# Softcapped attention and a gated MLP in one kernel: score tiles of 64 keys of two head pairs, 64x64 products, another order of steps

## The chip, the cores and the metric

The kernel runs on one core of a Trainium2 chip. The metric is device time in microseconds (us) of one execution. PE is TensorE, ACT is ScalarE, DVE is VectorE, POOL is GpSimd; SP issues transfers. L315 and the like are line numbers of the kernel before.

## The reference

```
q, k, v: (4, 12, 448, 64) float32; cap = 30; w_in (768, 2048), w_out (2048, 768)
scores = q @ k.T / sqrt(64)
scores = cap * tanh(scores / cap)
attn = exp(scores - max(scores))
attn = attn / (sum(attn) + 1e-9)
x = (attn @ v), heads side by side: (1792, 768)
h = x @ w_in
out = (h * sigmoid(h)) @ w_out
```

## The kernel before

The kernel has two parts: attention, then the MLP (called MoE in the code). Weights arrive as 64-bit floats and are turned into 32-bit ones by steps on DVE ("decode", lines L167 to L180).

**Attention.** Batch and heads make 24 head pairs; a *slot* s treats two pairs, t = 0 and 1, which is four heads, and there are 12 slots. A pair has its queries and keys, transposed, in one tile QK (128 partitions: head e of the pair on partitions 64e to 64e+63; three buffers), and its values in VT. The 448 keys of a head are cut into three chunks of 128 and a rest of 64.

- `qk(i, j)` (L315): the scores of pair i and key chunk j. Four products of 64x64 weights with 448 columns fill one score tile: partitions are the chunk's 128 keys, the two halves are the heads. `qk_rem(s)` (L327) does the last 64 keys of both pairs of the slot in one tile. Score tiles have three buffers of two PSUM banks each, and the tile of the sums takes one of them in turn.
- `tanh` (L337, L341) reads a score tile out of PSUM and writes the weights P; `exp` (L345) works in place: chunks 0 and 1 of a pair together (1792 elements a partition), chunk 2 (896), and the rest of both pairs (896).
- `pv(i, j)` (L378): values of a chunk, two products of 128x64 into the value tile O, one PSUM tile of two banks with a single buffer. `pv_rem` (L386): the rest, four products of 64x64.
- `sums` (L355, L360) adds the weights of the chunks on DVE into T, one tile a pair; `fold` (L390) adds the rest by two accumulating transfers on POOL's queue; `pv_sum` (L400) sums over the keys by products with a tile of ones, 128x32 each, into 448 columns of a score tile, two slots late.
- `u_vals` (L407) copies O out of PSUM, which frees it. `u_sums` (L415 to L429) turns the sums by a transpose on DVE, takes the reciprocal, turns them back, and sends them to the partitions of both halves by eight transfers. `norm` (L440 to L444) multiplies and writes the result as a high and a low part, XH and XL.

The order of attention is written out by hand. `SLOT` is a list of such steps, run for each slot; `-1` or `+1` behind a name is the slot before or the next one. Each engine has its own queue and takes its instructions in this order; what is late holds up what stands behind it on its engine. `ENDS` are lists for the last slots, into which six pieces of the MLP's first unit (H0 to H5) are put. `FIRST` says which slot does which decode step.

**MLP.** w_in is applied by a Strassen-like scheme (`chain`, L745), w_out by `o_unit` (L855). Each product is done as three, of high and low parts. PE's order here is a fixed line; `plan` orders the work of the other engines by costs and due times, from assumed times at which they come free. The result is added up in DRAM by accumulating transfers (L897).

Loads of QK, VT and the rest values VB are issued on POOL's queue (L299, L302, L306), those of the first slot on SP's.

Of the kernel before, what the change touches and what calls it, by code (L numbers as in the profile page):

```python
# [185 lines left out]
def tile_softcap_attention_swish_moe(  # L186
# [40 lines left out]
    W02 = [const.tile([128, 2 * DM], F32R, name=f"w{r}") for r in range(3)]  # L227
# [16 lines left out]
    QK = [a1.tile([128, S + KW], F32, name=f"QK{r}") for r in range(3)]  # L244
# [35 lines left out]
    O = {}  # L280
    U = {}
# [13 lines left out]
    def load_rem(b, eng=nc.gpsimd):  # L295
# [5 lines left out]
    def load_qk(i, eng=nc.gpsimd, c0=0, c1=S + KW):  # L301
        eng.dma_start(out=QK[i % 3][:, c0:c1], in_=qkv[i, :, c0:c1])  # L302

    def load_v(s, eng=nc.gpsimd):
        for t in range(2):
            eng.dma_start(out=VT[s % 2][:, t], in_=qkv[2 * s + t, :, S + KW:])  # L306

    def qk(i, j):

        q = QK[i % 3]  # L310
        ps = scores_tile()
        for c in range(2):
            for e in range(2):
                k0 = S + 128 * CHUNK[j] + 64 * c
                nc.tensor.matmul(  # L315
                    ps[half(c), e, 0:S], q[half(e), k0:k0 + 64], q[half(e), 0:S], start=True, stop=True
                )
        SP[i, j] = ps

    def qk_rem(s):  # L320

        ps = scores_tile()
        for t in range(2):
            q = QK[(2 * s + t) % 3]
            for e in range(2):
                k0 = S + KF + 64 * e
# [3 lines left out]
        SP[s, "r"] = ps  # L330

    def tanh(i, j):
        t = i % 2
        if (i, j // 2) not in P:
            P[i, j // 2] = a1.tile([128, 4 - j, S], F32, tag=f"P{t}{j // 2}", name="P")
        p = P[i, j // 2][:, 2 * (j % 2):2 * (j % 2) + 2]
        nc.scalar.activation(out=p, in_=SP.pop((i, j))[:, :, 0:S], func=AF.Tanh, scale=REG["sct"])  # L337

    def tanh_rem(s):
        P[s, "r"] = a1.tile([128, 2, S], F32, tag="PR", name="P", bufs=2)  # L340
        nc.scalar.activation(out=P[s, "r"], in_=SP.pop((s, "r"))[:, :, 0:S], func=AF.Tanh, scale=REG["sct"])  # L341

    def exp(i, h):
        p = P[i, h]
# [5 lines left out]
    def sums(i, n):  # L350

        p = P[i, n]
        if n == 0:
            T[i] = a1.tile([128, 2, S], F32, tag=f"T{i % 2}", name="T", bufs=2)
            nc.vector.scalar_tensor_tensor(  # L355
                out=flat(T[i]), in0=flat(p[:, 0:2]), scalar=epst[:, 0:1], in1=flat(p[:, 2:4]),
                op0=ALU.add, op1=ALU.add,
            )
        else:
            nc.vector.tensor_tensor(flat(T[i]), flat(T[i]), flat(p), ALU.add)  # L360

    CHUNK = (1, 2, 0)
    DONE = {}

    def summed(i):
        if i // 2 not in O:
            O[i // 2] = ps_o.tile([128, 2, 512], F32, tag="o", name="o")
        n = DONE[i] = DONE.get(i, 0) + 1
        return n == 1, n == KC + 1

    def pv(i, j):

        s, t = divmod(i, 2)
        start, stop = summed(i)
        for e in range(2):
            v = VT[s % 2][:, t, D * (e * KC + CHUNK[j]):D * (e * KC + CHUNK[j]) + D]
            p = P[i, j // 2][:, 2 * (j % 2) + e]
            nc.tensor.matmul(O[s][half(e), t, 0:S], v, p, start=start, stop=stop)  # L378

    def pv_rem(s):  # L380
        for t in range(2):
            start, stop = summed(2 * s + t)
            for e in range(2):
                v = VB[(s // NU) % 2][half(t), s % NU, e]
                p = P[s, "r"][half(t), e]
                nc.tensor.matmul(O[s][half(e), t, 0:S], v, p, start=start, stop=stop)  # L386

    def fold(s):
        for t in range(2):
            nc.gpsimd.dma_start(out=T[2 * s + t][half(t)], in_=P[s, "r"][half(t)], accum_op=ALU.add)  # L390

    def pv_sum(s, folded=True):

        ps = scores_tile()
        for z in (1,) if folded else (0, 1):
# [16 lines left out]
    def u_sums(s, parts=(0, 1, 2)):  # L412
        if 0 in parts:
            UW[s] = au.tile([128, S // 32, 32], F32, tag="US", name="US", bufs=2)
            nc.vector.transpose(flat(UW[s]), US.pop(s)[:, 0, 0:S])  # L415
        if 1 in parts:
            CW[s] = au.tile([128, S // 32], F32, tag="CS", name="CS", bufs=1)
            nc.vector.reciprocal(out=CW[s], in_=UW[s][:, :, 0])
        if 2 not in parts:
            return  # L420
        u = UW.pop(s)
        nc.vector.transpose(u, CW.pop(s).unsqueeze(2).to_broadcast([128, S // 32, 32]))
        rt = flat(u)

        r = au.tile([128, 2, S], F32, tag="R", name="R", bufs=2)
        for e in range(2):
            for h in range(2):
                for c in range(2):
                    nc.sync.dma_start(  # L429
                        out=r[64 * e + 32 * h:64 * e + 32 * h + 32, c], in_=rt[64 * e + 32 * c:64 * e + 32 * c + 32]  # L430
                    )
        RB[s] = r

    def norm(s, parts=(0, 1, 2)):
        b, u = s // NU, s % NU
        cs = slice(b * S, (b + 1) * S)
        x = U[s]
# [43 lines left out]

    def step(op, sh, slot):
        s = slot + sh
        if not 0 <= s < NS:
            return
        i = 2 * s + (1 if op[1:2] == "k" else 0)
        j = int(op[2]) if op[2:3].isdigit() else None
        if op == "SUM":
            pv_sum(s, s + 1 < NS)
        elif op == "UC":  # L490
            u_vals(s)
        elif op[:2] == "UT":
            u_sums(s, (j,))
        elif op[0] == "N":
            norm(s, (int(op[1]),))
        elif op[0] == "D":
            if (slot, op) in FIRST:
                decode(*FIRST[slot, op])
        elif op == "A":
            if s + 1 < NS:  # L500
                fold(s)
        elif op == "L1":
            if s + 1 < NS:
                load_qk(2 * s + 3)
# [824 lines left out]
```

## Time and profile before

| | |
|---|---|
| median of 3 runs | 606.33 us (605.38 to 607.08) |
| profiled execution | 605.26 us, span 603.4 us |
| granted clock of PE over the span | 0.999 |
| PE busy | 594.9 us (99%), 3578 products |
| DVE busy | 425.8 us (71%) |
| ACT busy | 370.0 us (61%) |
| POOL busy | 225.5 us (37%) |
| PE's first score product | 4.16 us |
| PE's first MLP product behind attention | 153.62 us |

Busy shares are means over both parts. In the page's slices ACT is at 9 tenths or more in nearly all of attention and at about 5 in the MLP, so attention has to be read by itself. A product of 32-bit numbers shows as two records on PE, one for each pass.

### The profile page before, as it was taken

The numbers are of one execution on the slowest core, as the hardware profiler recorded it, in microseconds if no ns is written. First come the engines' busy times: TensorE is split into PE (matmuls) and PEld (weight loads), VectorE is DVE, ScalarE is ACT, GpSimd is POOL, SyncE is SP. The second block draws the span as 40 slices with busy tenths as digits, with TensorE's granted clock in tenths as the row PEclk, the third lists the DMA queues.
The fourth block names the chain that finished last, engine by engine and source line by source line (L and its number), as shares of the span: only waits on it lengthen the run. The fifth ranks groups of instructions, "written<-read, shape, count | busy, mean of one in ns | idle before, by whom it ended". The sixth has DMA issues, their size and how long they took to land.

```text
span 603.4 us, 9839 instructions
## 1 busy us (share of the span) xinstructions
PE 594.9 (99%) x3578; PEld 477.8 (79%) x3578; DVE 425.8 (71%) x703; ACT 370.0 (61%) x602; POOL 225.5 (37%) x300
## 2 busy tenths in 40 slices
PE   7999999999999999999999999999999999999996
PEld 3333333334899999999999999999999999999996
DVE  2779888789888898766756585766676575747653
ACT  7999999997356565655655554645556555545120
POOL 2354433420043214433643463444335434635210
PEclk9999999999999999999999999999999999999999
DMA  7799999974394627988897899789898978998875
GB/s 249 209 221 215 256 209 183 239 161 66 67 309 122 209 100 140 141 172 184 120 202 97 181 138 201 101 192 147 158 175 127 200 103 178 134 198 138 287 244 199
DMA packets 46698, 105.13 MB, mean 174 GB/s; under 512 B 8018, under 2 KB 33746, under 8 KB 46642
## 3 DMA queue, kind: packets, MB, share of 16 engines
q0 software_dynamic: 33312, 67.62, 63.1%
q1 hardware_dynamic: 13330, 36.81, 18.1%
q8 instruction: 30, 0.49, 0.4%
q14 instruction: 26, 0.21, 0.1%
HBM read 47.97 MB, written 44.04 MB: 152 GB/s over the span
## 4 chain that ended last, share of the span: by engine, by line
PE 96%; ACT 2%; DVE 1%; issue 0%; ACTq 0%; DVEq 0%
PE q L855 38%; PE A L745 15%; PE C L745 10%; PE o L378 8%; PE s L315 8%; PE B L745 6%; PE D L745 4%; PE s L400 2%; PE o L386 1%; PE s L327 1%; ACT P L345 1%; ACT P L337 1%; PE s L745 1%; PE o L262 0%; DVE T L355 0%
## 5 line engine op out<-in xcount | busy, mean ns | idle before, releaser
L897 POOL DMA_DIRECT2D out_dram<-st x196 | 163.2, 964 | 252.4 <-ACT st L599 231.7
L855 PE MATMUL q<-w,gh 128*128 128x376 f32 (+1 forms) x876 | 187.6, 335 | 0.0
L855 PEld LDWEIGHTS q<-w,gh 128*128 128x128 f32 x876 | 156.4, 188 | 2.8
L599 ACT ACTIVATE st<-q 128x376 f32<-128x376 f32 (+1 forms) x184 | 82.6, 489 | 66.6 <-PE q L855 54.3
L855 PE MATMUL q<-w,gl 128*128 128x376 f32 (+2 forms) x438 | 111.3, 335 | 0.0
L855 PEld LDWEIGHTS q<-w,gl 128*128 128x128 f32 x438 | 80.2, 188 | 0.0
L345 ACT ACTIVATE P<-P 128x896 f32<-128x896 f32 (+1 forms) x60 | 71.2, 1259 | 0.0
L337 ACT ACTIVATE P<-s 128x896 f32<-128x896 f32 x72 | 62.4, 925 | 5.8 <-PE s L315 5.7
L315 PE MATMUL s<-QK 64*64 64x448 f32 x576 | 60.3, 545 | 2.1 <-ACT P L337 1.1
L745 PE MATMUL A<-XH,w 128*128 128x384 f32 (+1 forms) x192 | 60.5, 359 | 0.0
L378 PE MATMUL o<-P,VT 128*64 128x448 f32 x288 | 56.8, 543 | 0.0
L315 PEld LDWEIGHTS s<-QK 64*64 64x64 f32 x576 | 20.1, 133 | 39.5 <-issue 13.3
L599 ACT ACTIVATE gh<-gf 128x512 fp32r<-128x512 f32 (+1 forms) x63 | 36.3, 578 | 21.5 <-DVE gf L809 21.5
L815 DVE TENSOR_TENSOR gl<-gf,gh 128x512 fp32r<-128x512 f32 (+1 forms) x63 | 39.1, 622 | 13.3 <-ACT gh L599 13.2
L378 PEld LDWEIGHTS o<-P,VT 128*64 128x64 f32 x288 | 19.6, 137 | 36.0 <-issue 30.7
L599 ACT ACTIVATE gf<-A 128x512 f32<-128x512 f32 (+1 forms) x34 | 18.7, 549 | 42.6 <-PE A L745 39.6
L745 PE MATMUL C<-XH,w 128*128 128x384 f32 (+1 forms) x136 | 41.0, 363 | 0.0
L355 DVE SCALAR_TENSOR_TENSOR T<-P,epst 128x896 f32<-128x896 f32 x24 | 26.9, 1123 | 17.9 <-ACT P L345 17.9
L390 POOL DMA_DIRECT2D T<-P x22 | 18.6, 845 | 54.1 <-ACT P L345 34.8
L169 ACT ACTIVATE gf<-RAW 128x384 f32<-128x384 f32 x56 | 30.6, 548 | 13.1 <-DVE C L827 4.9
L745 PE MATMUL A<-xt,w 128*128 128x512 f32 (+1 forms) x168 | 38.3, 363 | 0.0
L745 PEld LDWEIGHTS A<-XH,w 128*128 128x128 f32 x192 | 35.6, 188 | 3.3
(136 smaller groups left out, 933.3 us busy)
## 6 DMA issues: line engine op xcount, KB each, us to landing
out_dram<-st POOLq DMA_DIRECT2D x98, 196.0 KB, 4.9
out_dram<-st POOLq DMA_DIRECT2D x98, 188.0 KB, 4.0
RAW<-in_moe_w_in_dram SPq DMA_DIRECT2D x15, 768.0 KB, 6.2
RAW<-in_moe_w_out_dram SPq DMA_DIRECT2D x14, 768.0 KB, 7.3
QK<-in_qkv_dram POOLq DMA_DIRECT2D x21, 480.0 KB, 5.2
R<-US SPq DMA_DIRECT2D x96, 56.0 KB, 4.1
T<-P POOLq DMA_DIRECT2D x22, 224.0 KB, 4.5
VT<-in_qkv_dram POOLq DMA_DIRECT2D x22, 192.0 KB, 4.6
```

Of the source, the lines that this page charges most:

```text
L169: nc.scalar.activation(out=tmp, in_=high.bitcast(F32), func=AF.Abs)
L315: nc.tensor.matmul(ps[half(c), e, 0:S], q[half(e), k0:k0 + 64], q[half(e), 0:S], start=True, stop=True)
L337: nc.scalar.activation(out=p, in_=SP.pop((i, j))[:, :, 0:S], func=AF.Tanh, scale=REG["sct"])
L345: nc.scalar.activation(out=p, in_=p, func=AF.Exp, scale=REG["cap"])
L355: nc.vector.scalar_tensor_tensor(out=flat(T[i]), in0=flat(p[:, 0:2]), scalar=epst[:, 0:1], in1=flat(p[:, 2:4]), op0=ALU.add, op1=ALU.add,)
L378: nc.tensor.matmul(O[s][half(e), t, 0:S], v, p, start=start, stop=stop)
L390: nc.gpsimd.dma_start(out=T[2 * s + t][half(t)], in_=P[s, "r"][half(t)], accum_op=ALU.add)
L599: nc.scalar.activation(out=out, in_=in_, func=AF.Copy)
L745: nc.tensor.matmul(ps, w(a), x(b), start=(first and z == 0), stop=(last and z == 2), skip_group_check=more)
L815: nc.vector.tensor_tensor(gl, gf, gh.bitcast(F32), ALU.subtract)
L855: nc.tensor.matmul(pe(e), g[a][:, ts], w[:, b, cols[e]], start=(z == 0 and a == 0 and b == 0), stop=(z == G - 1 and a == 1),)
L897: nc.gpsimd.dma_start(out=out[rows, part_cols(fp)[e]], in_=SUM[fp, blk, t, e], **how)
```

## The change

Attention is laid out anew. A score tile now holds the same 64 keys of two pairs: `qk(s, u)` has u from 0 to 6, and partitions 64t to 64t+63 are pair t. Products over keys therefore have 64 rows each: `pv(s, u)` does four of 64x64 for every u, and `pv_sum` four of 64x64 with a tile of ones that is 64 wide, which writes each sum to all 64 partitions of its head and needs no transfers behind it. The transposes of the sums are 896 wide, and the norm's first step reads O in PSUM directly; the copy `u_vals` is gone, and O is free when that step is done. The weights stand in groups of three, three and one u, and an exp treats a whole group (2688, 2688, 896 elements), except in the first and the last slot, where each u has its own. DVE adds five times a slot; u = 2 is added by one accumulating transfer of the full tile, in the first and last slot on DVE. There the sum also takes u = 6 by four more products.

QK has four buffers, and the loads of QK, VT and VB go to SP's queue. The start loads the first 512 columns of pair 0 on SP's queue and of pair 1 on ACT's. The order is written out for slots 0 to 4 (`START`) and 9 to 11 (`END`), with a repeated `SLOT` between. In the MLP the names of the first banks change, one weight tile moves to another pool, only the last slot's second and third norm steps are left to the planner, and its assumed start times are other ones.

```
-        for c in range(2):
-            for e in range(2):
-                k0 = S + 128 * CHUNK[j] + 64 * c
...
+        for t in range(2):
+            q = QK[(2 * s + t) % 4]
             for e in range(2):
+                k0 = S + 64 * u + (64 * e if u == NC - 1 else 0)
                 nc.tensor.matmul(
                     ps[half(t), e, 0:S], q[half(e), k0:k0 + 64], q[half(e), 0:S], start=True, stop=True
                 )
...
+    GROUPS = ((0, 1, 2), (3, 4, 5), (6,))
...
+    def fold(s):
+        t, p = T[s, 0], weights_of(s, 2)
+        if s not in EDGE:
+            nc.gpsimd.dma_start(out=t, in_=p, accum_op=ALU.add)
+        else:
+            nc.vector.tensor_tensor(flat(t), flat(t), flat(p), ALU.add)
...
+                p = weights_of(s, u)[half(t), e]
+                nc.tensor.matmul(O[s][half(e), t, 0:S], v, p, start=(DONE[s] == 0), stop=(DONE[s] == NC - 1))
...
+                    nc.tensor.matmul(
+                        ps[half(e), t, 0:S], ones[half(t)], p[half(t), e], start=(n == 0), stop=(n == len(parts) - 1)
+                    )
...
-    def u_vals(s):
-        U[s] = au.tile([128, 2, S], F32, tag="U", name="U", bufs=3)
-        nc.vector.tensor_copy(U[s], O.pop(s)[:, :, 0:S])
...
-            nc.vector.tensor_tensor(flat(x), flat(x), flat(RB.pop(s)), ALU.mult)
+            nc.vector.tensor_tensor(x, O.pop(s)[:, :, 0:S], RB.pop(s), ALU.mult)
...
     SLOT = """
-        Er-1 Sk0-1 Vi1-1 Ti2 Vk2-1 N0-4 Ti0 Vk1-1 Ti1 N1-4 Vk0-1 Sk1-1 Ei1 SUM-2 A-1 Ei0 Qk2 UT0-2 D1 Qr Tk2 N2-4 Vr-1 L1
...
+        T1 UT2-2 E2-1 Q4 Q3 LV-1 S1-1 N0-2 V3-1 Q5 V5-1 T4 S4-1 A0-1 V6-1 D2 E0 S2-1 N1-2 S3-1 N2-3 V0-1 V1-1 T3
...
+        load_qk(0, 0, S + 64)
+        load_qk(1, 0, S + 64, nc.scalar)
+        nc.sync.dma_start(out=cap0, in_=cap.partition_broadcast(1))
...
+        load_qk(0, S + 64, S + KW)
+        load_qk(1, S + 64, S + KW)
+        load_v(0)
...
-        free = {"PE": 0.0, "ACT": 3.2, "DVE": 4.5, "POOL": 0.0, "SP": 9.5}
+        free = {"PE": 0.0, "ACT": 2.1, "DVE": 2.8, "POOL": 0.0, "SP": 0.0}
```

What the new lists make of the engines' queues shows at three places. First PE in a middle slot. Before (s are scores, o values; a number is the buffer):

```order
L315 MATMUL s<-QK_85 64x448 x8
L315 MATMUL s<-QK_83 64x448 x12
L378 MATMUL o<-P,VT_87 64x448 x12
L400 MATMUL s<-T,ones 32x448 x4
L315 MATMUL s<-QK_84 64x448 x4
L327 MATMUL s<-QK_83 64x448 x2
L327 MATMUL s<-QK_84 64x448 x2
L386 MATMUL o<-P,VB_89 64x448 x4
```

The same engine and part of a slot after, where L327 is `qk`, L387 `pv` and L397 `pv_sum`:

```order
L387 MATMUL o<-P,VT_87 64x448 x4
L327 MATMUL s<-QK_82 64x448 x2
L327 MATMUL s<-QK_83 64x448 x2
L387 MATMUL o<-P,VT_87 64x448 x4
L387 MATMUL o<-P,VB_89 64x448 x4
L387 MATMUL o<-P,VT_87 64x448 x8
L397 MATMUL s<-T,ones 64x448 x4
L387 MATMUL o<-P,VT_87 64x448 x4
L327 MATMUL s<-QK_82 64x448 x2
L327 MATMUL s<-QK_83 64x448 x2
L327 MATMUL s<-QK_84 64x448 x2
L327 MATMUL s<-QK_85 64x448 x2
```

Before, scores, values and sums stand in blocks; after, single tiles of scores and values alternate, and a score tile takes its four products from two QK buffers. The second place is ACT at the start, before (L337 and L341 are tanh, L345 exp):

```order
L337 ACTIVATE P<-s 128x896 x2
L270 ACTIVATE epst<-over_60 1x1
L290 TENSOR_LOAD cap_92
L337 ACTIVATE P<-s 128x896
L345 ACTIVATE P<-P 128x896
L345 ACTIVATE P<-P 128x1792
L337 ACTIVATE P<-s 128x896
L341 ACTIVATE P<-s 128x896
```

And after (L336 is tanh, L340 exp), from the second tanh on:

```order
L336 ACTIVATE P<-s 128x896 x2
L340 ACTIVATE P<-P 128x896
L336 ACTIVATE P<-s 128x896 x4
L340 ACTIVATE P<-P 128x896 x3
L336 ACTIVATE P<-s 128x896 x2
L340 ACTIVATE P<-P 128x896
L336 ACTIVATE P<-s 128x896
L340 ACTIVATE P<-P 128x896
L336 ACTIVATE P<-s 128x896 x3
L340 ACTIVATE P<-P 128x2688 x2
L336 ACTIVATE P<-s 128x896 x4
```

In these rows are the rest of slot 0, six tanh of slot 1 and its two long exps; the first tanh of the last row is the second one of slot 2. The third place is DVE in a middle slot, before:

```order
L415 STREAM_TRANSPOSE US<-s 128x448
L176 SCALAR_TENSOR_TENSOR KRV<-RAW_66,KRV 128x768
L444 TENSOR_TENSOR XL<-U,XH 128x2x448
L418 RECIPROCAL CS<-US 128x14
L355 SCALAR_TENSOR_TENSOR T<-P,epst 128x896
L407 COPY U<-o 128x896
L422 STREAM_TRANSPOSE US<-CS 128x448
L360 TENSOR_TENSOR T<-T,P 128x896
```

And after (L408 and L414 are the transposes, L425 the norm's first step, L363 the sum that joins both halves and takes in the fold):

```order
L408 STREAM_TRANSPOSE US<-s 128x896
L411 RECIPROCAL CS<-US 128x28
L171 TENSOR_SCALAR KRV<-KRV 128x768
L172 TENSOR_SCALAR KRV<-KRV 128x768
L414 STREAM_TRANSPOSE US<-CS 128x896
L361 TENSOR_TENSOR T<-P 128x896
L425 TENSOR_TENSOR U<-o,US 128x896
L365 TENSOR_TENSOR T<-T,P 128x896
L176 SCALAR_TENSOR_TENSOR KRV<-RAW_66,KRV 128x768
L365 TENSOR_TENSOR T<-T,P 128x896
L427 CAST XH<-U 128x2x448
L363 TENSOR_TENSOR T<-T 128x896
```

The copy L407 is gone, and L425, which reads the value tile, stands behind the second transpose and a sum.

## Rows read from the trace of the kernel before

**Rows 1.** The page, costliest groups: busy, mean ns of one, idle before
```profile
L855 PE MATMUL q<-w,gh 128*128 128x376 f32 (+1 forms) x876 | 187.6, 335 | 0.0
```

**Rows 2.** Timeline of PE: start us, us, line, records; start and end of attention
```profile
4.16 2.75 PE L315 MATMUL s<-QK 64*64 64x448 f32 x24
7.72 0.98 PE L315 MATMUL s<-QK 64*64 64x448 f32 x8 [0.81 <-DMA QK<-in_qkv_dram]
...
25.99 4.73 PE L378 MATMUL o<-P,VT 128*64 128x448 f32 x24
...
153.62 0.45 PE L745 MATMUL C<-XH,w 128*128 128x384 f32 x1
```

**Rows 3.** Timeline of PE, one slot
```profile
66.72 0.98 PE L315 MATMUL s<-QK 64*64 64x448 f32 x8
67.52 0.93 PE L327 MATMUL s<-QK 64*64 64x448 f32 x8
68.27 0.93 PE L386 MATMUL o<-P,VB 64*64 64x448 f32 x8
69.02 3.94 PE L315 MATMUL s<-QK 64*64 64x448 f32 x40
72.89 4.73 PE L378 MATMUL o<-P,VT 128*64 128x448 f32 x24
77.55 0.96 PE L400 MATMUL s<-T,ones 128*32 128x448 f32 x8
78.44 0.98 PE L315 MATMUL s<-QK 64*64 64x448 f32 x8
```

**Rows 4.** Timeline of ACT in the same slot
```profile
71.63 3.38 ACT L345 ACTIVATE P<-P 128x896 f32<-128x896 f32 x3
74.90 2.54 ACT L337 ACTIVATE P<-s 128x896 f32<-128x896 f32 x3
77.29 2.56 ACT L345 ACTIVATE P<-P 128x896 f32<-128x896 f32 x2
79.72 0.94 ACT L337 ACTIVATE P<-s 128x896 f32<-128x896 f32 x1
```

**Rows 5.** Timeline of DVE in the same slot
```profile
66.86 0.65 DVE L415 STREAM_TRANSPOSE US<-s 128x448 f32<-128x448 f32 x1 [0.56 <-PE s L400]
67.43 0.55 DVE L167 TENSOR_SCALAR KRV<-RAW 128x768 uint32<-128x768 uint32 x1
...
70.09 0.24 DVE L418 RECIPROCAL CS<-US 128x14 f32<-128x14 f32 x1
70.24 1.08 DVE L355 SCALAR_TENSOR_TENSOR T<-P,epst 128x896 f32<-128x896 f32 x1
71.23 1.09 DVE L407 COPY U<-o 128x896 f32<-128x896 f32 x1
...
74.20 1.15 DVE L355 SCALAR_TENSOR_TENSOR T<-P,epst 128x896 f32<-128x896 f32 x1 [0.36 <-ACT P L345]
75.27 1.08 DVE L440 TENSOR_TENSOR U<-U,R 128x896 f32<-128x896 f32 x1
76.39 0.63 DVE L442 CAST XH<-U 128x896 fp32r<-128x896 f32 x1
...
79.15 0.93 DVE L176 SCALAR_TENSOR_TENSOR KRV<-RAW,KRV 128x768 uint32<-128x768 uint32 x1
```

**Rows 6.** Groups of instructions by line: weight loads of the 64x64 value units
```profile
L386 PEld LDWEIGHTS o<-P,VB 64*64 64x64 f32 x96 | 3.6, 133 | 5.6 <-issue 5.6
```

**Rows 7.** Timeline of ACT, the first tanh
```profile
5.48 1.73 ACT L337 ACTIVATE P<-s 128x896 f32<-128x896 f32 x2 [3.22 <-PE s L315]
```

**Rows 8.** DMA issues: count, KB each, median us to landing
```profile
QK<-in_qkv_dram POOLq DMA_DIRECT2D x21, 480.0 KB, 5.2
...
T<-P POOLq DMA_DIRECT2D x22, 224.0 KB, 4.5
...
xt<-XL POOLq DMA_DIRECT2D x1, 512.0 KB, 7.4
```

More of the change, by code (lines that the diff above doesn't have):

```diff
@@ L226, in tile_softcap_attention_swish_moe @@
     RAW = [const.tile([128, 2 * DM], F32, name=f"RAW{r}") for r in range(NBUF)]
-    W02 = [const.tile([128, 2 * DM], F32R, name=f"w{r}") for r in range(3)]
+    W02 = [const.tile([128, 2 * DM], F32R, name=f"w{r}") for r in range(2)]
     att = ExitStack()
@@ L243, in tile_softcap_attention_swish_moe @@
     NU = NP // 2
-    QK = [a1.tile([128, S + KW], F32, name=f"QK{r}") for r in range(3)]
+    QK = [a1.tile([128, S + KW], F32, name=f"QK{r}") for r in range(4)]
     VT = [a1.tile([128, 2, 2 * KC * D], F32, name=f"VT{r}") for r in range(2)]
@@ L329, in qk_rem, with tanh, exp @@
                 )
[L330 to L344, printed above, removed]
+        SP[s, u] = ps
+    def tanh(s, u):
+        g, k = place(u)
+        if (s, g) not in P:
+            P[s, g] = a1.tile([128, len(GROUPS[g]), 2, S], F32, tag=f"P{g}", name="P", bufs=2 if g < 2 else 1)
+        nc.scalar.activation(out=P[s, g][:, k], in_=SP.pop((s, u))[:, :, 0:S], func=AF.Tanh, scale=REG["sct"])
+    def exp(s, g, k=None):
+        p = (P[s, g] if k is None else P[s, g][:, k:k + 1]).rearrange("p u a s -> p (u a s)")
         nc.scalar.activation(out=p, in_=p, func=AF.Exp, scale=REG["cap"])
@@ L348, in flat, with weights_of, sums @@
         return t.rearrange("p a s -> p (a s)")
-    def sums(i, n):
-        p = P[i, n]
+    def weights_of(s, u):
+        g, k = place(u)
+        return P[s, g][:, k]
+    def sums(s, n):
+        if n == 2 and s in EDGE:
+            return
+        p = lambda u: flat(weights_of(s, u))
         if n == 0:
-            T[i] = a1.tile([128, 2, S], F32, tag=f"T{i % 2}", name="T", bufs=2)
+            T[s, 0] = a1.tile([128, 2, S], F32, tag="Ta", name="T", bufs=2)
             nc.vector.scalar_tensor_tensor(
-                out=flat(T[i]), in0=flat(p[:, 0:2]), scalar=epst[:, 0:1], in1=flat(p[:, 2:4]),
-                op0=ALU.add, op1=ALU.add,
-            )
-        else:
-            nc.vector.tensor_tensor(flat(T[i]), flat(T[i]), flat(p), ALU.add)
@@ L362, in tile_softcap_attention_swish_moe @@
[L362 to L378, printed above, removed]
@@ L380, in pv_rem @@
-    def pv_rem(s):
+                out=flat(T[s, 0]), in0=p(0), scalar=epst[:, 0:1], in1=p(1), op0=ALU.add, op1=ALU.add
+            )
+        elif n == 1:
+            T[s, 1] = a1.tile([128, 2, S], F32, tag="Tb", name="T", bufs=2)
+            nc.vector.tensor_tensor(flat(T[s, 1]), p(3), p(4), ALU.add)
+        elif n == 3:
+            nc.vector.tensor_tensor(flat(T[s, 0]), flat(T[s, 0]), flat(T[s, 1]), ALU.add)
+        else:
+            nc.vector.tensor_tensor(flat(T[s, 1]), flat(T[s, 1]), p({2: 6, 4: 5}[n]), ALU.add)
@@ L388, in fold @@
[L388 to L395, printed above, removed]
+                if u == NC - 1:
+                    v = VB[(s // NU) % 2][half(t), s % NU, e]
+                else:
+                    d0 = D * (e * KC + u // 2)
+                    v = VT[s % 2][half(t), u % 2, d0:d0 + D]
+                p = weights_of(s, u)[half(t), e]
@@ new lines, in u_sums @@
+    def u_sums(s, part):
+        n = 2 * S // 32
+        if part == 0:
+            UW[s] = au.tile([128, n, 32], F32, tag="US", name="US", bufs=1)
+            nc.vector.transpose(UW[s].rearrange("p (a k) n -> p a (k n)", a=2), US.pop(s)[:, :, 0:S])
+        elif part == 1:
+            CW[s] = au.tile([128, n], F32, tag="CS", name="CS", bufs=1)
+            nc.vector.reciprocal(out=CW[s], in_=UW[s][:, :, 0])
+        else:
+            u = UW.pop(s)
+            nc.vector.transpose(u, CW.pop(s).unsqueeze(2).to_broadcast([128, n, 32]))
+            RB[s] = u.rearrange("p (a k) n -> p a (k n)", a=2)
@@ L436, in norm @@
         cs = slice(b * S, (b + 1) * S)
+        if 0 in parts:
+            U[s] = au.tile([128, 2, S], F32, tag="U", name="U", bufs=2)
         x = U[s]
@@ L496, in step @@
         elif op[0] == "D":
-            if (slot, op) in FIRST:
-                decode(*FIRST[slot, op])
-        elif op == "A":
+            if (s, op) in FIRST:
+                decode(*FIRST[s, op])
+        elif op[0] == "A":
+            fold(s)
+        elif op == "LQ":
+            if s + 2 < NS:
+                load_qk(2 * s + 4)
+                load_qk(2 * s + 5)
+            for m in WANTED:
+                load_w(m)
+            WANTED.clear()
+        elif op == "LV":
             if s + 1 < NS:
[L501 to L504, printed above, removed]
@@ L1220, in moe @@
             sums(fp)
-        for s, at in ((NS - 3, 0.0), (NS - 2, 9.5), (NS - 1, 13.5)):
-            op(("x", s), "DVE", 2.9, lambda s=s: norm(s), [("x", s - 1)], at=at)
+        op(("x", NS - 1), "DVE", 1.75, lambda: norm(NS - 1, (1, 2)))
         for c in range(2):
```

229 lines of the change are left out of this document (114 added, 115 removed).

## The prediction

> **What bounds the kernel now.** The page comes first: PE is busy 99% of the span, so the question is whether its time is work or loss. In the costliest groups of the page the products of the MoE part have 0.0 us of idle time before them (one such row stands in [rows 1]), and PE's order of that part is the same in both kernels: it can only lose. What the change can win lies between PE's first score product at 4.16 and its first gated-MLP product behind attention at 153.62 us [rows 2].
>
> There PE's timeline shows one slot (four heads) in 11.72 us [rows 3]. I call 448 columns through the whole array a unit: four 64x64 products or two 128x64 ones. The reader is to see that two units of 64x64 tiles, of different lines (the scores of the last keys, then their values), begin 0.75 us apart (67.52, 68.27, 69.02), whereas at each change of tile shape time is missing: five score units up to the values take 3.87 (0.12 over 5 x 0.75), six value units up to the sums 4.66 (0.16 over), the sum 0.89 (0.14 over), the first score unit 0.80 (0.05 over). A slot is 15 units = 11.25 plus 0.47 for three changes of shape (64x64, 128x64, 128x32). PE has no other gap there.
>
> Then the other engines in the same slot, since PE's bound is only 0.4 us wide. ACT [rows 4]: three tanh start 0.797 apart (74.90 to 77.29); a pair of exps over 896 and 1792 elements takes 2.43 (77.29 to 79.72), the three from 71.63 take 3.27, so 896 costs 0.84 and 1792 costs 1.59. Seven tanh, three short and two long exps: 5.58 + 2.52 + 3.18 = 11.28 of 11.72. DVE [rows 5]: a sum over 896 costs 0.99 (70.24 to 71.23), a 448-wide transpose 0.57 (66.86 to 67.43), the reciprocal 0.15 (70.09 to 70.24), the cast of the norm 0.6, decode steps 0.55 and 0.93. The norm's product took 1.12 where its result was read at once (75.27 to 76.39); it and the difference I take at 1.0, as operations over 896 like the sum. ACT and DVE stand close behind PE.
>
> **The change, part by part.** *Shapes.* Values and sums become 64x64 products, so the three shape changes go. Per slot there are still 15 units, by the 0.75 of the 64x64 value unit in [rows 3] 11.25 to 11.27 us: 0.45 less. Slots 0 and 11 sum in two units, so 182 units instead of 181: +0.75. The weight loads of a value unit double: in the 64x64 value unit of before they are there (133 ns each, x96) [rows 6], and its pace is still 0.75, so I cost them at nothing; if they did show, each pass would cost 0.13 more, see the rivals. The Trainium skill says ("TensorE: Matmul & The Clock Gate", Part 3, The mechanism) that a weight load overlaps running matmuls only where the row group differs. In a value unit two column tiles share a row group. By that rule the sum would be some 22 us worse; by the row it is not, and the trace disagrees with the rule here.
>
> *ACT.* Exps come as 2688, 2688 and 896 elements: 0.84 + 2 x 0.747 = 2.34 for the long ones. A slot is 5.58 + 4.68 + 0.84 = 11.10. The second long exp stands directly behind the tanh whose output it reads: between nothing and 0.15 (a tanh takes 0.94 but lets the next start after 0.80). Taken at 0.15: 11.25, just under PE's 11.27.
>
> *DVE.* Out: four sums at 0.99, the copy. In: five sums at 0.99 and transposes of 896 columns. These are not in the trace: between 0.57 (no dearer) and 1.14 (twice); I take 1.04, as an 896-wide operation costs about 0.47 more than a 448-wide one, and 0.1 more for the first, whose result is read at once. 5 x 0.99 + 2.08 + 0.1 + 0.15 + 1.0 + 0.6 + 1.0 = 9.9, plus decode: by 0.55 for a step on integers and 0.93 for an or-step or a difference, 1.5 us in slots 5 and 6, 2.0 in slot 7, 0.9 in slot 8. So 11.4, 11.4, 11.9, 10.8 against 11.27: DVE falls some 0.9 us behind in slots 5 to 7. What waits is PE's first value unit, since the value tile has one buffer and is now freed only by the norm's first step (before, by the copy). A lead of that step takes up the first tenths, so I count 0.6 of it on PE, and 0.4 for the edges: 1.0 us of such waits in the sum, between nothing (transposes no dearer) and 1.7.
>
> *The start.* Score units of slot 0 need two head pairs at once. Before, the first needed 288 KB and began at 4.16, the next needed pair 1 and waited until 7.72, by when 960 KB had been asked for and landed (288, 192 and 480, by the columns of the loads) [rows 2]; ACT, which began its tanh at 5.48 [rows 7], had three tanh of pair 0 to fill the time. Now the first unit needs two pieces of 256 KB, the second two more of 224 KB: again 960 KB, one piece issued from ACT's queue. The second unit can begin between 5.7 (nothing contends) and 7.7; I take 7.2, because SP still queues the pieces one behind the other. Its tanh starts 1.0 later, at 8.2. From there ACT has no gap: ahead of the tanh that frees the score tile of PE's 26th unit stand 12 tanh, 6 exps of 896 and 2 of 2688: 9.6 + 5.0 + 4.7 = 19.3. It starts at 27.5, ends 0.94 later, and PE goes on at 28.6 with 25 units done. Before, 24 units were done at 25.99 [rows 2]. So the start loses 2.6 us.
>
> *The rest.* From there 157 units and the first unit of the MLP remain in both. Before, they took 153.62 - 25.99 = 127.6, with the three shape changes of eleven slots among them: 11 x 0.47 = 5.2. Now they are gone and the 1.0 of waits comes: 123.4. That saves 4.2.
>
> *Moved and removed transfers.* Loads of Q, K, V go from POOL's queue to SP's, where only waits for free buffers stand ahead of them; with four Q/K buffers they lead their use by a slot (11 us, against a landing of 5.2 us [rows 8]): nothing, and if the lead were gone each microsecond late would be one on PE. The 96 small copies of the reciprocals go (448 KB a slot). One fold of 448 KB takes the place of two of 224 KB; it no longer has a slot's slack, see the rivals. The MLP head, its gates and one norm instead of three in the MoE's first stretch change nothing that PE waits for.
>
> *Sum.* -4.2 + 2.6 = -1.6. The profiled execution took 605.26 us (1.86 beside its span), 1.07 under the median 606.33. So 603.7 on its scale, **604.7** against the median.
>
> **Rivals.** What a measurement can tell here is about 0.3%, 1.8 us.
> 1. *The start isn't late.* If the pieces land by 5.7, ACT's chain is bound by its own first tanh and exp instead: the second tanh at 7.4, PE on at 27.8; with DVE's waits gone too, -3.4: 602.9. For it: DMA has spare capacity in the first microseconds; against: pair 1 waited until 7.72. 16 in 100.
> 2. *DVE becomes the bound.* One sum in [rows 5] (74.20) took 1.07 to the next start, not 0.99. Five such a slot add 0.4: 10.2 plus decode, 11.7 in the slots with 1.5 us of decode, so most of the 0.45 is gone there and kept only in about five slots: 2.3 saved, 2.6 lost: 606.6, no change. 14 in 100.
> 3. *Slower: the fold's landing.* The loop is: first sum of a slot (1.1), fold landing L after its issue, joining sum (1.0), third norm step behind it on DVE (1.0), first sum of the next slot. Its length is L + 3.1, so from L = 8.2 on the slot is longer than 11.27, and every further microsecond costs one in each of ten slots. Folds of 224 KB land in 4.5 us, an accumulating copy of 512 KB in 7.4 [rows 8]. 448 KB between them is under 8.2, but queued among the loads it may not be. At L = 8.7: +5, so 609.7. 8 in 100.
> 4. *The change doesn't do what it says.* If the 0.15 belongs to a change of what is multiplied, not of shape, the eight changes between scores, values and sum in the new slot would cost 1.2, 0.73 more than the three of now: 11 x 0.73 + 2.6 = +10.6: 617. Against it: 67.52, 68.27, 69.02 in [rows 3]. 2 in 100.
> 5. *Weight loads show.* 84 value units x 2 passes x 0.133 = 22 us: 627. This is what the rule of the Trainium skill named above would do here; [rows 6], with 0.75 a unit, speaks against it. 2 in 100.
>
> **How the numbers follow.** My forecast has 58 in 100, with its own range 603.6 to 605.8 (second unit between 6.5 and 7.7; DVE waits 0.4 to 1.7). Its edge at 1.8 us cuts it: 24 of the 58 are faster by over 0.3%, 34 within. Faster: 24 + 16 = 40. Same: 34 + 13 of rival 2 = 47. Slower: 8 + 2 + 2 + 1 = 13. The range takes in rival 2, nearly all of rival 1 and leaves out the slow ones: 602.5 to 607.0.
>
> **What would show it.** Right: in a middle slot, score, value and sum units all 0.75 apart in PE's timeline, slot 11.25 to 11.35; the 26th unit waits for ACT and begins near 28.6; the MLP's first products behind attention near 152. Wrong: a sum unit or first value unit waiting for DVE by more than 0.5 in each slot (rival 2), joining sums idle until the fold's DMA (rival 3), or starts 0.9 apart at score-to-value changes (rivals 4, 5). The forecast fails most easily in the start, whose landing times I only bounded.

## The result, and the profile after

The changed kernel takes **611.2 us** (median of 6 runs, 610.66 to 611.58); the kernel before took 605.51 in the same job. The ratio is 1.0088 [1.0075 to 1.0101]: slower by 0.9%, outside the predicted range, where a gain of 1.6 us was forecast. The profiled execution has a span of 609.5 us. First comes PE's timeline of the changed kernel, at the start of attention, around the joining sum of slot 1, and at the end; it answers to [rows 2].

```profile
4.70 4.47 PE L327 MATMUL s<-QK 64*64 64x448 f32 x32 [0.49 <-DMA QK<-in_qkv_dram]
10.82 1.79 PE L327 MATMUL s<-QK 64*64 64x448 f32 x16 [1.65 <-ACT P L336]
...
30.19 2.60 PE L327 MATMUL s<-QK 64*64 64x448 f32 x24 [1.56 <-ACT P L336]
...
42.07 1.05 PE L397 MATMUL s<-T,ones 64*64 64x448 f32 x8 [4.02 <-DVE T L363]
42.84 1.77 PE L327 MATMUL s<-QK 64*64 64x448 f32 x8
44.32 2.69 PE L387 MATMUL o<-P,VT 64*64 64x448 f32 x16
...
159.35 0.44 PE L760 MATMUL D<-XH,w 128*128 128x384 f32 x1
```

The last row is the MLP's first product behind attention: 159.35, against 153.62 in [rows 2], 5.7 later. What follows it to the end of the span is 450.15 us, against 449.78 before, so nearly the whole loss is made in attention. Two places stand out: the 26th unit starts at 30.19 instead of the 28.6 of the forecast, and at 42.07 a sum has waited 4.02 us for DVE.

Next, one middle slot in the same view; it answers to [rows 3].

```profile
65.58 0.96 PE L397 MATMUL s<-T,ones 64*64 64x448 f32 x8
66.34 0.96 PE L387 MATMUL o<-P,VT 64*64 64x448 f32 x8
67.09 1.71 PE L327 MATMUL s<-QK 64*64 64x448 f32 x16
68.59 0.96 PE L387 MATMUL o<-P,VT 64*64 64x448 f32 x8
69.34 3.21 PE L327 MATMUL s<-QK 64*64 64x448 f32 x32
...
76.86 0.96 PE L397 MATMUL s<-T,ones 64*64 64x448 f32 x8
```

Read the starts: sum, value, two scores, value, four scores lie 0.75 a unit apart, whatever follows what, and from sum to sum is 11.28 us (11.72 before). The saving of 0.44 a slot is there, and no row of PE shows a wait between 49 us and the end of attention. ACT and DVE of the same slot, in the answer to [rows 4, 5]:

```profile
64.67 1.75 ACT L336 ACTIVATE P<-s 128x896 f32<-128x896 f32 x2
...
75.96 1.75 ACT L336 ACTIVATE P<-s 128x896 f32<-128x896 f32 x2
```

```profile
66.70 1.11 DVE L408 STREAM_TRANSPOSE US<-s 128x896 f32<-128x896 f32 x1
67.84 0.33 DVE L411 RECIPROCAL CS<-US 128x28 f32<-128x28 f32 x1
...
68.91 1.09 DVE L414 STREAM_TRANSPOSE US<-CS 128x896 f32<-128x896 f32 x1
69.92 1.05 DVE L361 TENSOR_TENSOR T<-P 128x896 f32<-128x896 f32 x1
```

ACT's slot is 11.29 (11.25 was worked out), and in the rows of that slot ACT has no idle time. The 896-wide transposes take 1.14 and 1.01 to the next start (1.04 + 0.1 and 1.04).

**Why the 26th unit is late.** The timeline of SP, ACT and DVE at the start, in order of time:

```profile
4.01 0.45 SPq L546 DMA_DIRECT2D cap<-in_cap_dram  x1
...
6.03 0.92 ACT L336 ACTIVATE P<-s 128x896 f32<-128x896 f32 x1 [3.38 <-PE s L327]
...
8.27 0.14 DVE L272 TENSOR_SCALAR epst<-cap 1x1 f32<-1x1 f32 x1 [3.12 <-DMA cap<-in_cap_dram]
...
8.63 0.20 ACT L275 ACTIVATE epst<-cap 1x1 f32<-1x1 f32 x1 [1.60 <-DVE cap L273]
9.01 0.95 ACT L340 ACTIVATE P<-P 128x896 f32<-128x896 f32 x1 [0.18 <-ACT epst L275]
9.87 1.71 ACT L336 ACTIVATE P<-s 128x896 f32<-128x896 f32 x2
```

The change adds a second copy of the cap on partition 64. Its 4-byte load goes out at 4.01, behind the first Q, K and V pieces, and is there at 8.27, 4.2 us later. ACT's own small exp of it stands ahead of the first exp and of the second tanh in ACT's order, so the second tanh starts at 9.87 where 8.2 was forecast.

**Why the sum waits.** The chain of work that ended last, of the stretch from 28 to 50 us, and who issued what at its head (timelines of SP and POOL):

```profile
29.21 11.57 DMA T<-P
...
40.88 1.10 DVE T L363
41.98 0.09 issue
42.07 1.05 PE s L397 x8
```

```profile
28.66 0.81 SPq L308 DMA_DIRECT2D QK<-in_qkv_dram  x2
29.56 0.38 SPq L606 DMA_DIRECT2D RAW<-in_moe_w_out_dram  x1
29.99 1.27 SPq L313 DMA_DIRECT2D VT<-in_qkv_dram  x2
...
29.21 1.04 POOL L370 DMA_DIRECT2D T<-P  x1 [28.31 <-DVE T L356]
```

The fold of slot 1 takes 11.57 us to land. It goes out while SP issues five loads: Q and K of slot 3 (2 x 480 KB), a block of w_out (768 KB) and V of slot 2 (2 x 192 KB), 2.1 MB. In the DMA view the ten folds of the kernel have this median:

```profile
T<-P POOLq DMA_DIRECT2D x10, 448.0 KB, 6.0
```

so it is this one that is late, not all ten. The next slowest are those of slots 7 and 8, with 7.9; the view around the first of them, which goes out at 101.70:

```profile
T<-P POOLq DMA_DIRECT2D x1, 448.0 KB, 7.9
```

Behind the wait comes a third thing. The windows of the changed kernel, then those of a variant (e10, below) in which PE works through the wait; after the engines' busy times come PE's granted clock, the DMA share and GB/s:

```profile
43.00:44.00 1.00, 1.00 (x12) 0.47 (x8) 1.00 (x3) 1.00 (x1) 0.39 (x1) 0.50 0.00 0
44.00:45.00 1.00, 1.00 (x8) 0.32 (x4) 0.93 (x3) 0.44 (x2) 0.49 (x1) 0.50 0.00 0
45.00:46.00 1.00, 1.00 (x12) 0.51 (x8) 1.00 (x1) 0.62 (x1) 0.00 (x0) 0.50 1.09 208
46.00:47.00 1.00, 1.00 (x16) 0.50 (x12) 1.00 (x2) 0.00 (x0) 0.00 (x0) 0.87 1.19 158
```

```profile
42.00:43.00 1.00, 1.00 (x16) 0.40 (x12) 1.00 (x3) 1.00 (x1) 0.00 (x0) 1.00 0.06 16
43.00:44.00 1.00, 1.00 (x16) 0.37 (x12) 1.00 (x2) 1.00 (x2) 0.88 (x1) 1.00 0.00 0
44.00:45.00 1.00, 1.00 (x16) 0.46 (x12) 0.93 (x3) 0.47 (x1) 0.00 (x1) 1.00 0.84 73
```

PE came back from 4.02 us of idling and was granted 0.50, the level of 1.2 GHz, from 43 to 46 us. The unit at 42.84 takes 1.48 to the next start, the two at 44.32 take 2.47: 3.95 for three units that take 2.25 elsewhere, 1.7 us.

### The profile page after: what moved, and what is told of

The parts are those of the page before. It is cut to its first block, busy times and chain, and to the rows that moved or that the text cites. A ratio compares the mean times of both kernels' runs of the same rounds, so it can differ in the third digit from the quotient of the medians.

```text
span 609.5 us, 10200 instructions
## 1 busy us (share of the span) xinstructions
PE 594.5 (98%) x3874; PEld 487.4 (80%) x3874; DVE 441.4 (72%) x714; ACT 366.9 (60%) x578; POOL 183.8 (30%) x227
## 4 chain that ended last, share of the span: by engine, by line
PE 89%; DVE 4%; DMA 3%; ACT 2%; issue 1%; SPq 0%; DVEq 0%; ACTq 0%
PE q L870 37%; PE A L760 14%; PE o L387 9%; PE C L760 8%; PE s L327 8%; PE B L760 6%; PE D L760 3%; DMA T<-P 2%; PE s L397 2%; ACT P L336 1%; ACT P L340 1%; PE s L760 1%; DMA cap<-in_cap_dram 1%; DVE xt L694 1%; DVE US L408 0%
## 5 line engine op out<-in xcount | busy, mean ns | idle before, releaser
L613 ACT ACTIVATE st<-q 128x376 f32<-128x376 f32 (+1 forms) x177 | 80.3, 488 | 61.3 <-PE q L870 48.3
L336 ACT ACTIVATE P<-s 128x896 f32<-128x896 f32 x84 | 72.8, 936 | 9.6 <-PE s L327 6.6
L327 PE MATMUL s<-QK 64*64 64x448 f32 x672 | 73.0, 547 | 4.5 <-ACT P L336 4.1
L340 ACT ACTIVATE P<-P 128x896 f32<-128x896 f32 (+1 forms) x44 | 71.6, 1653 | 0.5 <-ACT epst L275 0.2
L387 PE MATMUL o<-P,VT 64*64 64x448 f32 x576 | 64.3, 544 | 0.0
L327 PEld LDWEIGHTS s<-QK 64*64 64x64 f32 x672 | 26.4, 134 | 44.3 <-ACT P L336 21.5
L760 PE MATMUL A<-XH,w 128*128 128x512 f32 (+1 forms) x192 | 61.2, 362 | 0.0
L387 PEld LDWEIGHTS o<-P,VT 64*64 64x64 f32 x576 | 23.9, 135 | 31.8 <-issue 29.0
L370 POOL DMA_DIRECT2D T<-P x10 | 8.7, 871 | 126.9 <-DVE T L356 93.0
L760 PE MATMUL B<-XH,w 128*128 128x384 f32 (+1 forms) x136 | 40.5, 359 | 0.0
L760 PE MATMUL C<-XH,w 128*128 128x512 f32 (+1 forms) x124 | 37.7, 365 | 0.0
```

The costliest lines, as they stand in the source:

```text
L327: nc.tensor.matmul(ps[half(t), e, 0:S], q[half(e), k0:k0 + 64], q[half(e), 0:S], start=True, stop=True)
L336: nc.scalar.activation(out=P[s, g][:, k], in_=SP.pop((s, u))[:, :, 0:S], func=AF.Tanh, scale=REG["sct"])
L340: nc.scalar.activation(out=p, in_=p, func=AF.Exp, scale=REG["cap"])
L370: nc.gpsimd.dma_start(out=t, in_=p, accum_op=ALU.add)
L387: nc.tensor.matmul(O[s][half(e), t, 0:S], v, p, start=(DONE[s] == 0), stop=(DONE[s] == NC - 1))
L613: nc.scalar.activation(out=out, in_=in_, func=AF.Copy)
```

## The experiments

All of them edit the changed kernel; ratios are to the kernel before, run on the same chip.

**e1: the 4-byte load early.**

```diff
         nc.sync.dma_start(out=cap0, in_=cap.partition_broadcast(1))
+        nc.sync.dma_start(out=cap64[64:65], in_=cap.partition_broadcast(1))
...
         load_v(0)
-        nc.sync.dma_start(out=cap64[64:65], in_=cap.partition_broadcast(1))
```

> Only the 4-byte load of cap for partition 64 moves up, right behind the first load of cap. Theory (the changed start waits for this load): in the changed kernel ACT stood idle 1.60 us from 7.03 because the second tiny exp waited for DVE and DVE for this load, issued at 4.01 and landed at 8.2; now it is issued near 1.7 and lands before 6, so the second tanh of the start moves from 9.87 to about 8.2 and PE's 26th unit from 30.19 to about 28.6; the fold of slot 1 still lands late, so the whole is 611.2 - 1.6 = 609.6. Rival (the Q/K pieces of pair 1 hold up the start anyway): ACT's idle time stays and the time stays at 611.2.

Measured 610.54 us, 1.0081 [1.0064 to 1.0098]. ACT no longer waits for the cap. Its PE timeline:

```profile
28.42 2.60 PE L327 MATMUL s<-QK 64*64 64x448 f32 x24 [1.21 <-ACT P L336]
...
39.88 1.77 PE L397 MATMUL s<-T,ones 64*64 64x448 f32 x8 [3.60 <-DVE T L363]
```

The 26th unit comes at 28.42, near the forecast's 28.6, which was worked out without the cap's chain. The sum still waits 3.60 (fold 10.8 us) and the clock is 0.50 from 40 to 42. In the profiled execution attention ends 2.0 earlier than in the changed kernel (157.31); in the median 0.7, within the two intervals. Only with the fold's wait gone (e2 against e5) does the load's share stand out.

**e2: the fold of slot 1 as an addition on DVE**, as the kernel does in its first and last slots.

```diff
-        if s not in EDGE:
+        if s not in EDGE + (1,):
             nc.gpsimd.dma_start(out=t, in_=p, accum_op=ALU.add)
```

> Only the fold of slot 1 is done by DVE, as in slots 0 and 11, in place of the transfer. Theory (the late landing of this one fold, 11.6 us after its issue, costs PE 4.0 us at the sum of slot 1 and ACT and PE some 2 us behind it): no wait of the joining sum, PE's sum unit of slot 1 at about 38.0 instead of 42.07, and 611.2 - 5.8 = 605.4. Rival (the wait only hides another one, DVE's extra 1.0 us or the next score tile): less than 2 us come back, above 609.

Measured 607.56, 1.0036 [1.0024 to 1.0049], 3.6 us under the changed kernel (5.8 were expected). The sum of slot 1 starts at 37.61 with no wait, the clock stays at 1.00. Now the fold of slot 2 is late (9.7 us) and its sum waits 1.82.

**e3: the block of w_out out of the burst**, the loads that slots 0 and 1 would have asked for here asked for in slot 2.

```diff
-            for m in WANTED:
+            for m in WANTED if s > 1 else ():
                 load_w(m)
-            WANTED.clear()
+            WANTED[:] = WANTED if s <= 1 else []
```

> Only the 768 KB load of a w_out block, which went out at 29.56 beside the fold of slot 1, is issued a slot later. Theory (the fold queues behind loads that were issued before it; the DMA engines moved some 270 KB a us from 30 to 39): 768 KB less to move, the fold lands about 2.8 us sooner, the sum's wait falls from 4.0 to about 1.2, 608.4. Rival (the first accumulating transfer of a program is slow by itself): it still lands after 11 to 12 us, 611.2.

Measured 608.17, 1.0042 [1.0028 to 1.0057]. With 768 KB of 2.1 MB gone the fold lands in 9.2 instead of 11.6, the sum waits 1.65, and the clock behind it stays at 1.00.

**e4: an earlier, small accumulating transfer**, into a tile that nothing uses yet, ahead of the first fold.

```diff
+        nc.gpsimd.memset(KRV, 0.0)
+        nc.gpsimd.dma_start(out=KRV[:, 0:64], in_=ones, accum_op=ALU.add)
```

> Adds one small accumulating transfer on POOL's queue in the first microseconds, into a scratch tile that is overwritten later, so that the fold of slot 1 is no longer the first of its kind. Theory (queueing behind loads): nothing changes, the fold lands after 11 to 12 us, 611.2. Rival (first use is slow): the fold lands after 5 to 7 us and 5 us come back, 606.

Measured 611.56, 1.0087 [1.0068 to 1.0106]; the fold takes 11.2, the sum waits 3.68. That it is the first of its kind does not make it late.

**e5: the edits of e1 and e2 together.**

> Both repairs: the load of cap for partition 64 early, and the fold of slot 1 on DVE. Theory (the two waits are the whole loss): the MLP begins behind attention near 152 to 153.6, 155.2 of the run with the fold alone less 1.6, and 605.3 to 606; the fold of slot 2 may still land late (9.7 us in that run, 1.8 us of wait), and if that wait shrinks too, 604. Rival (the early load brings nothing, since ACT's start is then bound by data): as with the fold alone, 607.5.

Measured 605.97 (10 runs), 1.0011 [1.0002 to 1.0021]. The time is as expected. Against e2 the two ratios give the 4-byte load's share by itself: 1.5 us, as the 1.6 of the timeline. The 26th unit starts at 28.39; the fold of slot 2 (9.8 us) makes its sum wait 1.85.

**e6: two changes of shape put back**, the sums as eight 64x32 products.

```diff
-                    nc.tensor.matmul(
-                        ps[half(e), t, 0:S], ones[half(t)], p[half(t), e], start=(n == 0), stop=(n == len(parts) - 1)
-                    )
+                    for c in range(2):
+                        r = slice(64 * e + 32 * c, 64 * e + 32 * c + 32)
+                        nc.tensor.matmul(
+                            ps[r, t, 0:S], ones[half(t), 0:32], p[half(t), e], start=(n == 0), stop=(n == len(parts) - 1)
+                        )
```

> The changed kernel with the sum's four 64x64 products cut into eight of 64x32, the same result and the same columns through the array; only two changes of tile shape a slot come back. Theory (each change of shape costs PE some 0.15 us, whatever is multiplied): a middle slot of 11.57 instead of 11.27, and some 3 us more in all, 614. Rival (what was saved came from the layout or the order, not from the shapes): a middle slot of 11.27 and 611.2.

Measured 612.25, 1.0117 [1.01 to 1.0134]. PE's timeline around one sum:

```profile
61.25 1.68 PE L387 MATMUL o<-P,VT 64*64 64x448 f32 x16
62.86 0.98 PE L399 MATMUL s<-T,ones 64*32 64x448 f32 x16
63.77 0.98 PE L387 MATMUL o<-P,VT 64*64 64x448 f32 x8
64.58 1.68 PE L327 MATMUL s<-QK 64*64 64x448 f32 x16
```

Two value units in front take 1.61 instead of 1.50, the sum 0.91, the value unit behind 0.81: 0.33 more a slot, and the slot from sum to sum is 11.60. That is 0.16 a change of shape, as read from [rows 3]. The whole kernel lost less than the 3 us expected, 1.05 by the medians and 1.8 by the ratios: in the profiled execution its fold landed in 10.4, the sum waited 2.92 and the clock stayed at 1.00, so some of the other loss was missing there.

**e8: the 4-byte load early (e1), folds of slots 1 and 2 on DVE. e9: e8, and the block of w_out asked for in slot 3** (the last two edits, e9 alone).

```diff
-        if s not in EDGE:
+        if s not in EDGE + (1, 2):
...
-            for m in WANTED:
+            for m in WANTED if s > 2 else ():
                 load_w(m)
-            WANTED.clear()
+            WANTED[:] = WANTED if s <= 2 else []
```

> As the two repairs, with the fold of slot 2 on DVE too, 1.0 us more of DVE's time there. Theory (late landings are what costs, and DVE has room in slot 2): no sum unit waits for a transfer, the MLP begins near 152.2 and the time is 604.1, 0.2% under the kernel before. Rival (DVE becomes the bound of slot 2): the value unit behind it waits by up to 1.0, 605.

> As the kernel with two folds on DVE, and the 768 KB load of a w_out block in slot 3 instead of slot 1. Theory (with no fold to hold up, that load delays nothing in slots 1 and 2): the same as without it, 604.1, or up to 0.5 slower if the fold of slot 3 now queues behind it. Rival (the load also delays Q, K and V that PE waits for): 0.5 to 1 us faster.

Measured 605.52, 0.9997 [0.9987 to 1.0007], and 605.4, 0.9999 [0.999 to 1.0009], 10 runs each. The sum of slot 2 waits 0.30 in both. In e9 the 26th unit comes at 28.54 and the MLP at 153.56 (153.62 in [rows 2]). Both missed the 604.1 expected. In e8 the 26th unit comes later, at 29.40, as the last piece of pair 1 lands at 8.0 there (7.0 in e9) and the second tanh, at 9.06, waits 0.47 for its scores. The repairs bring the kernel back to the time before, not under it.

**e10: PE busy during the wait**, with products that nothing reads, ahead of the sum of slot 1 and in its tile.

```diff
+        for _ in range(5 if s == 1 else 0):
+            for t in range(2):
+                for e in range(2):
+                    nc.tensor.matmul(
+                        ps[half(e), t, 0:S], ones[half(t)], QK[t][half(t), 0:S], start=True, stop=True
+                    )
```

> The changed kernel, with five units of products (3.75 us) that nothing uses put on PE ahead of the joining sum of slot 1, into the sum's own tile, so that PE is busy in most of its 4.0 us wait there. Theory: the half clock behind that sum comes from PE's idle time. Then the sum still starts at about 42.0, when the fold has landed, the clock stays at 1.00 behind it, and the MLP's first product comes about 1.7 us earlier: 157.6, time about 609.5 (ratio to before 1.006). Rival: the half clock belongs to something else that falls on the same microseconds, such as the loads or ACT's burst behind the fold: the clock is 0.50 for some 3 us all the same, and the time stays at 611.2.

The mechanism came out, the saving only in part. The fold is as late (10.9), the sum starts at 41.78, and the clock behind it is 1.00 (the windows above), with units at 0.75: the half clock came from PE's idling. The MLP starts at 158.18, 1.2 before the changed kernel's, and 0.9 of that lies behind the sum; a new wait of 0.6 at the sum of slot 7 (109.75) took back most of the rest of the 1.7. The profile puts it down to ACT, but DVE's joining sum ended last there, at 109.65, after it had waited 1.48 for its fold, which took 8.8. The median, 611.43, 1.0093 [1.0076 to 1.011], missed the 609.5 expected and does not resolve a gain of this size.

**e11: the burst behind the fold.** The five loads go out on POOL's queue behind the fold of slot 1, and the first score unit of slot 3 moves behind the sum.

```diff
-        LQ.1 Q2.2 T2.2 ...
+        Q2.2 T2.2 ...
-        Q3.2 LV.1 S2.1 V2.1 S4.1 Q2.3 A0.1 V6.1 S3.1 SUM.1 T3.2 ...
+        Q3.2 S2.1 V2.1 S4.1 A0.1 LQ.1 LV.1 V6.1 S3.1 SUM.1 Q2.3 T3.2 ...
```

> The changed kernel, with the five loads that slots 0 and 1 ask for around 28.7 to 30.8 (2.1 MB: Q and K of slot 3, two expert weights, V of slot 2) put behind the fold of slot 1, on POOL's own queue, so that the fold goes out first; the first score unit of slot 3 moves behind the joining sum. Theory: the fold is late because it queues behind that burst. Then it lands in 4.5 to 6.5 us instead of 11.6, the sum of slot 1 doesn't wait and the clock stays at 1.00: 5 to 6 us less, unless the score unit of slot 3 now waits for its Q and K by 1 to 3 us: 606 to 609. Rival: this fold is slow by itself, wherever the loads stand (as it is the first of its queue, or by the reads of the two tiles): it takes 9 us or more again and the time stays near 611.

Measured 607.48 (10 runs), 1.002 [1.0009 to 1.0031]. The start of this profiled execution was late (26th unit at 31.47, as ACT waited 2.41 for the cap, whose load is as it was), and the fold went out at 30.48. Its DMA view and PE's timeline:

```profile
QK<-in_qkv_dram POOLq DMA_DIRECT2D x2, 480.0 KB, 7.4
RAW<-in_moe_w_out_dram POOLq DMA_DIRECT2D x1, 768.0 KB, 10.7
T<-P POOLq DMA_DIRECT2D x1, 448.0 KB, 6.8
```

```profile
38.53 0.98 PE L398 MATMUL s<-T,ones 64*64 64x448 f32 x8
```

The same loads are in flight beside the same fold, but it lands in 6.8 instead of 11.6, the sum does not wait, and the clock is 1.00 throughout. From the 26th unit to the MLP (156.16) it takes 124.7 us, against 129.2 in the changed kernel. The edit changes the queue of the loads along with their order. That the order is enough is seen in the changed kernel's own folds, with all loads on SP's queue. The first load goes out 0.55 ahead of the fold in slot 1, which takes 11.6; 0.20 and 0.05 behind it in slots 7 and 8, 7.9 each; about 0.8 behind it in slots 4 to 6, 6.0 each (in slot 6 with the same 2.1 MB as in slot 1); and 1.0 to 2.5 behind it in slots 2, 3 and 10, 4.4 to 5.3. In slot 9 two loads alone go out 1.8 and 1.4 ahead, and it takes 6.8. It is the order of issue that makes the fold late.

**e12: the edits of e1 and e2, and that of e9 on the block of w_out; the fold of slot 2 is a transfer.**

> Three repairs of the changed kernel at once: the 4-byte load early, the fold of slot 1 as an addition on DVE, and the second expert's output weights loaded in slot 3 instead of slot 1; the fold of slot 2 is a transfer again. Theory: with these weights out of the way the fold of slot 2 lands in 6 to 7 us and its sum waits for under 0.5 us (it waited 1.85 without the third repair), and DVE adds one fold less than in the kernel with two: 604.8 to 605.4 against 605.4 of before, ratio 0.998 to 1.000. Rival: what is left is not these waits but the dearer first 28 us: 605.4 to 606, no gain over the kernel with two folds on DVE.

A miss: 606.48 (12 runs), 1.0011 [1.0 to 1.0023], as e5. Without that block the fold of slot 2 still takes 9.7 and its sum waits 1.75. It is issued on POOL from 38.06 to 39.10, and SP issues Q and K of slot 4 from 38.27: loads again go out while the fold does. In the changed kernel the same fold went out at 43.61, the next load 1.0 behind it, and landed in 5.3.

## Why the prediction was wrong

**Right.** *Shapes*: the slot is 11.28 (11.25 to 11.27 worked out), e6 puts 0.33 of it back with two changes of shape, and the rest, without the two losses below, comes within 1.3 us of the forecast's 123.4 in e11 (124.7) and within 1.6 in e9 (125.0). Rivals 4 and 5 are refuted by 0.75 a unit at every pairing of lines; the rule of the Trainium skill ("TensorE: Matmul & The Clock Gate", Part 3, The mechanism), that a weight load overlaps running products only where the row group differs, is not borne out here either, as value units with two column tiles in a row group take 0.75. *ACT's slot* and *the transposes* were right to 0.04 and 0.03. Rival 2 did not come: in the middle slots one value unit alone, at 106.41, starts late for DVE, by 0.24.

**Failed: the start.** "From there ACT has no gap" took for the second tanh a start of 8.2 and counted what stands ahead of it, but left out the new load of the cap and the two small DVE steps and the small exp that hang on it; the step stood in the diff. It cost 1.6 in the timeline (30.19 for 28.6) and 1.5 by e2 against e5. With it gone, the 26th unit comes at 28.39 to 28.77 in e1, e5, e9 and e12 and at 29.40 in e8, and from the second tanh to it are 20.3 to 20.5 in each, the forecast's 20.4. That its 8.2 for the second tanh was near is in part luck. It was worked out as a wait for PE's second unit, forecast at 7.2 and seen at 6.70 in the changed kernel. In e1 and e9 the second tanh (7.97 and 8.20) stands right behind ACT's first tanh, two small exps and first exp and waits for no scores: that is the bound of rival 1, which had it at 7.4. In e5 and e8 it did wait for them, 0.28 and 0.47.

**Failed: moved transfers at nothing, and the fold's bound.** Costing SP's loads at "nothing" asked only whether they come in time, not what they do to a fold that is issued among them. Its landing was bounded by 4.5 and 7.4 and measured 11.6. The trace of before held a warning, in the landings of its 22 folds of half the size:

```profile
DMA to landing us min/median/max: 4.1/4.5/7.2
```

The forecast took the median; one of them had already needed 7.2. Rival 3 named this mechanism ("queued among the loads it may not be" under 8.2) at 8 in 100, but had the price recur in ten slots; it fell on slot 1 alone, for 4.0 us, as the other nine landed in 4.4 to 7.9, under its 8.2. The bound itself held: behind the two folds of 7.9 no sum of PE waits, behind those of 8.5 and 8.8 in e9 (below) two do. In slot 1, and in slot 2 of the repaired kernels, the loads are issued just ahead of the fold or during its issue. In e11 they come behind it, and in slot 6 a burst of the same 2.1 MB on SP's queue begins at 90.62, 0.8 behind the fold's 89.83, and that fold lands in 6.0.

**Missing from every case: the clock.** A wait of 4 us on PE did not cost its length alone: 1.7 more by the records. What of that stays to the end is 0.9 in e10's profile and not resolved in the medians.

**The sum in the trace.** 28.6 + 123.4 = 152.0 was forecast for the MLP; 1.6 + 4.0 + 1.7 = 7.3 leads to 159.3, and 159.35 was measured. That it closes so well is luck in part: of the 1.0 that the 123.4 holds for waits on DVE, 0.24 came (106.41), and late starts of at most 0.2 each, which nobody counted, make up the rest. 0.4 more lies behind attention.

**What stays open.** e9 has neither loss and still does not show the forecast's gain of 1.6: its stretch from 28.54 takes 125.0. PE starts 2.2 us late there in all, in small pieces (0.49 at the sum at 47.59, 0.47 and 0.39 at the sums of slots 7 and 8, 0.30 at 99.8, and 0.55 below 0.25 each up to that first sum), where 1.0 was counted; the other 0.4 lies in starts that are late by 0.14 or less. DVE's joining sums and PE's sums of slots 7 and 8 in e9:

```profile
103.60 1.09 DVE L363 TENSOR_TENSOR T<-T 128x896 f32<-128x896 f32 x1 [1.15 <-DMA T<-P]
104.80 0.98 PE L397 MATMUL s<-T,ones 64*64 64x448 f32 x8 [0.28 <-issue]
116.10 1.09 DVE L363 TENSOR_TENSOR T<-T 128x896 f32<-128x896 f32 x1 [0.49 <-DMA T<-P]
117.30 0.98 PE L397 MATMUL s<-T,ones 64*64 64x448 f32 x8 [0.21 <-issue]
```

So 0.86 of the 2.2 is the loss of slot 1 again, in small: these two folds landed in 8.5 and 8.8, with the first load 0.14 and 0.02 behind them. At 99.8 the value unit waits for DVE's norm step, which is the wait that the forecast did count. At 47.59 DVE's joining sum stands behind DVE's own work, to which the repair adds one addition; no run separates that from waits that the changed order has by itself, and in no run are the folds of slots 7 and 8 repaired.

## What to carry to other kernels

A transfer that takes part in a chain is priced by what is issued just ahead of it and while it is issued, and not by its median landing: here the same 448 KB took 4.4 to 11.6 us. The smallest line of a diff counts too: 4 bytes that an engine needs ahead of its next long step cost 1.5 us here. A median says little of the one transfer that goes out among others: read the largest landing too. Price a wait on PE of several microseconds with the clock behind it, and look for the few slots in which the steady state does not hold yet.

## What the hardware showed that was not expected

- Behind idle times of PE of 4.02, 3.60 and 3.68 us (the changed kernel, e1, e4) 3, 2 and 6 rows of 1 us show a granted clock of 0.50; behind 2.92 and 1.65 (e6, e3) it stayed at 1.00, as it did in e10, where PE worked through the wait.
- A 4-byte load issued behind six pieces of Q, K and V (1.3 MB in all) landed 4.2 us after its issue.
- A fold of 448 KB landed in 4.4 to 5.3 where the next load went out 1.0 us or more behind it (slots 2, 3 and 10 of the changed kernel), in 6.8 ahead of 2.1 MB on the same queue (e11), in 7.9 to 9.8 where Q and K went out on SP's queue 0.02 to 0.21 behind it (slots 7 and 8; slot 2 in e2, e5 and e12), and in 9.2 to 11.6 where they went out 0.55 ahead of it (slot 1 in the changed kernel, e1, e3, e4 and e10).
